# Windowed attention and gated projections: low parts of w_val summed on TensorE, x of seven groups copied to SBUF, a new order

## The chip, the cores and the metric

The kernel runs on one core of a Trainium2 chip. The core has five engines that work side by side, each with its own queue of instructions which it takes strictly in order: PE (TensorE, matrix products), DVE (VectorE), ACT (ScalarE), POOL (GpSimd) and SP, which here only issues transfers. Matrix products are written to PSUM; DVE and ACT read PSUM, and POOL's instructions in this kernel work on SBUF alone. The metric is the device time of one execution in microseconds (us), as a median of runs.

## The reference, cut to what matters

Two stages follow one another. Attention over 4 batches, 8 heads, 768 positions and head size 64, in which a query sees the first 8 keys and the 96 latest, with a bias that falls with the distance:

```python
scores = scale * np.matmul(q, k.transpose(0, 1, 3, 2))
scores = np.where(keep, scores + bias, -1000000000.0)
a = np.exp(scores - np.max(scores, axis=-1, keepdims=True))
a = a / (np.sum(a, axis=-1, keepdims=True) + 1e-09)
x = np.matmul(a, v)          # then heads side by side: x is [4, 768, 512]
```

Then a gated projection, with a causal convolution of five taps along the sequence as the gate:

```python
for k in range(K):
    gate_pre += conv_w[k] * xp[:, k:k + S, :]   # xp: x behind K - 1 rows of zeros
gate = 1.0 / (1.0 + np.exp(-gate_pre))
out = (gate * (x @ w_val)) @ w_out
```

The weights come as 64-bit floats, two 32-bit words each, and the result is float32.

## The kernel before, in words

**Groups, steps, phases.** The work is cut into 32 groups (batch, half of the sequence, pair of heads). A group has three steps of 128 queries. Four groups, the four head pairs of one half sequence, make a phase; there are eight. A group computes x transposed: 128 rows (two heads of 64) by 384 positions.

**A group's way through the engines.** `scores` (L406, PE) writes q times k. `add_bias` (L414, DVE) adds the bias and takes the minimum of the negated scores. `expo` (L424, ACT) takes the exponential and its sum. `guard` (L431, POOL or DVE), `recip` (L434, DVE) and `norm` (L439, POOL or DVE) normalise. `transpose` (L449 to L455, PE) and `evac_pt` (L149 on ACT, L151 on DVE: the helper `copy`) turn the probabilities. `pv` (L473 to L480, PE) multiplies by v into x, which has one PSUM bank (`X_B` is 1). Then all of these read x in that bank: `x_high` (a copy rounded to fp32r, L149 or L151), `x_low` (the rest, L556, DVE), five taps of the convolution into `gate` (the first at L566 on ACT or L568 on DVE, the others at L564 on DVE) and a copy of the last four positions to `hist` for the next half. `hist_in` writes four positions ahead of x (a memset at L548, or a copy from `hist`). Only when all of them are done is the bank free for the next group.

**A phase's projections.** `sigmoid` (L599, ACT), then `val` (L606): for each of four output blocks four times three products in fp32r, high by high, low by high and high by low, 384 columns each. `gated` (L613, DVE) multiplies by the gate, `g_high` and `g_low` (L619, POOL or DVE) split the product, and `outp` (L626) makes 36 products of 512 columns. `evac_o` copies the result out of PSUM and `store` (L637, SP) sends it. `val` and `outp` share two PSUM banks with the tag `moe`.

**The weights.** w_val and w_out are eight blocks of 128 by 512. Each is loaded as integers and taken apart: `f64_abs` (L305, ACT), five operations of `f64_op` on DVE (L313 clamps at F64_MIN; L315, L319, L322 and L325 work on bits and on the low word, L325 giving the remainder `r`), `w_high` (L149, rounds to fp32r), `w_rest` (L344, subtracts it) and `w_low` (L348, adds `r`), the last two on POOL or DVE.

**What sets the order.** No loop orders the queues. Each operation is added to a `Plan` with an urgency (its due time, counted in steps), a cost for each engine that may do it, and what it depends on. `Plan.order` simulates the engines: it picks for each operation that is ready the engine with the earliest end by the plan's costs plus that engine's entry in `SPARE` (L101), finds the operation that can start first, and gives its engine the most urgent one ready by then (L104). The program is written out in that order. `ring` makes an operation wait for the release of a buffer. The constants at L17 to L26 hold most urgencies: `W_AT` for the weight blocks, `U_XH`, `U_CV` and `CV_STEP` for the halves of x and the taps, `U_AM` to `U_EV` for a step's operations, `U_MOE` for the projections. `zeros` (L239) issues products that nobody reads, eight at the start (`WARM`) and one a step in the first `FILL_TO` groups. The load of group g's q and k is due at 3g - 12, of its v at 3g - 6, of a weight block 4 ahead of its `W_AT`.

Of the kernel before, what the change touches and what calls it, by code (L numbers as in the profile page):

```python
# [126 lines left out]
def attention_moe(ctx, tc, qT, kT, kg, vw, v0, v, counts_in, wv, cw, wo, out):  # L127
# [31 lines left out]
    ident = const.tile([P, P], F32, name="ident")  # L159
    rel = one.tile([P, WIN], F32, name="rel")  # L160
# [100 lines left out]
    plan.add(("IOTA",), -100, {POOL: 2.0}, iotas)  # L261

# [44 lines left out]
    def f64_op(raw, n, nm, k):  # L307
        lo, hi = raw[:, :, 0], raw[:, :, 1]
        y = T[nm, "y"][:, :n]
        yi = y.bitcast(I32)  # L310
        ve = nc.vector
        if k == 0:
            ve.tensor_scalar(out=y, in0=y, scalar1=F64_MIN, scalar2=None, op0=ALU.max)  # L313
        elif k == 1:
            ve.tensor_scalar(out=yi, in0=yi, scalar1=3, scalar2=0x3FFFFFF8,  # L315
                             op0=ALU.logical_shift_left, op1=ALU.bitwise_and)
        elif k == 2:
            h = tile_of((nm, "h"), [P, DM], I32, "wh", WT_B)[:, :n]
            ve.scalar_tensor_tensor(out=h, in0=hi, scalar=-0x40000000, in1=yi,  # L319
                                    op0=ALU.bitwise_and, op1=ALU.bitwise_or)  # L320
# [141 lines left out]
    def pv(g):  # L462
        for k in range(HB):
# [31 lines left out]
    def pv_deps(g):  # L495
        deps = [("EV", 3 * g + k) for k in range(HB)] + [("HI", g), ("LV", g)]
        return deps + ([("LV0", g)] if groups[g][1] == 0 else [])


    for g in range(NGRP + LAG):  # L500
        h = g - LAG
        if g < NGRP and g < ALONE:
            plan.add(("S", g), 3 * g, {PE: s_cost(g) + 2 * SWITCH}, lambda e, g=g: scores(g), s_deps(g))
        if 0 <= h and g < ALONE or g >= NGRP:
            plan.add(("PV", h), 3 * g, {PE: pv_cost(h) + 2 * SWITCH}, lambda e, h=h: pv(h), pv_deps(h))
        if ALONE <= g < NGRP:
            plan.add(("PV", h), 3 * g, {PE: pv_cost(h) + SWITCH}, lambda e, h=h: pv(h), s_deps(g) + pv_deps(h))
            plan.add(("S", g), 3 * g, {PE: s_cost(g) + 2 * SWITCH}, lambda e, g=g: scores(g), s_deps(g) + [("PV", h)])
            plan.follow(("S", g), ("PV", h))

    for g, (b, hf, p) in enumerate(groups):
        for k in range(HB):
# [20 lines left out]
            for j in range(2):  # L533
                plan.add(("NM", s, j), s + U_RC + 0.1, {POOL: 0.46 if full else 0.3, DVE: 0.25 if full else 0.15},
                         lambda e, s=s, j=j: norm(e, s, j), [("RC", s)])
# [7 lines left out]

    def hist_in(e, g):
        b, hf, p = groups[g]
        x = tile_of(("x", g), [P, HIST + HT], F32, "x", X_B, psum)
        if hf == 0:
            nc.vector.memset(x[:, :HIST], 0.0)  # L548
        else:
            copy(e, x[:, :HIST], hist[:, p])  # L550

    def x_high(e, g):
        copy(e, tile_of(("xh", g), [P, HT], F32R, "xh", XH_B), T["x", g][:, HIST:])

    def x_low(g):
        nc.vector.tensor_sub(tile_of(("xl", g), [P, HT], F32R, "xl", XH_B), T["x", g][:, HIST:], T["xh", g])  # L556

    def conv(e, g, k):
# [3 lines left out]
        gt, src, w = T["gate", ph][:, p], T["x", g][:, k : k + HT], cwt[:, p, k : k + 1]  # L562
# [4 lines left out]
        else:  # L567
            nc.vector.tensor_scalar(out=gt, in0=src, scalar1=w, scalar2=None, op0=ALU.mult)  # L568

    for g, (b, hf, p) in enumerate(groups):  # L570
        u = 3 * (g + LAG) + 1 + U_XE
        ph = g // NP
        key = ("HI", g)
        last = [("XL", g), ("CV", g, TAPS - 1)] + ([("HO", g)] if hf == 0 else [])
        plan.add(key, 3 * (g + LAG) - 2, {DVE: 0.08, ACT: 0.2} if hf else {DVE: 0.08}, lambda e, g=g: hist_in(e, g),
                 plan.ring("x", X_B, key, last) + ([("HO", g - NP)] if hf else []))
        if hf == 0:
            plan.add(("HO", g), u + 0.5, {ACT: 0.2, DVE: 0.08},
                     lambda e, g=g, p=p: copy(e, hist[:, p], T["x", g][:, HT:]),
                     [("PV", g)] + ([("HI", g - NP)] if g >= 2 * NP else []))  # L580
        key = ("XH", g)
        plan.add(key, u + U_XH, {ACT: 0.4, DVE: 0.47}, lambda e, g=g: x_high(e, g),
                 [("PV", g)] + plan.ring("xh", XH_B, key, [("VM", ph, NC - 1, p)]))
        key = ("XL", g)
        plan.add(key, u + U_XH + 0.1, {DVE: 0.48}, lambda e, g=g: x_low(g),
                 [("XH", g)] + plan.ring("xl", XH_B, key, [("VM", ph, NC - 1, p)]))
        for k in range(TAPS):
            key = ("CV", g, k)
            deps = [("PV", g), ("CW",)] + ([("CV", g, k - 1)] if k else [("HI", g)])
# [4 lines left out]
            plan.add(key, u + U_CV + CV_STEP * k, {DVE: 0.53} if k else {DVE: 0.53, ACT: 0.5},  # L594
# [45 lines left out]
    plan.ring("moe", 2, ("WARM",), [("WARM",)] + [("F", s) for s in range(3 * FILL_TO)])  # L640
    for ph in range(NPH):
        u = ph * PHS + U_MOE
        plan.add(("SG", ph), u - 1, {ACT: 4.0}, lambda e, ph=ph: sigmoid(ph),
                 [("CV", ph * NP + p, TAPS - 1) for p in range(NP)])
        for m in range(NC):
            for c in range(NC):
# [3 lines left out]
                plan.add(key, u + 6.0 * (4 * m + c) / 16, {PE: 0.53}, lambda e, ph=ph, m=m, c=c: val(ph, m, c), deps)  # L650
            key = ("GM", ph, m)
            plan.add(key, u + 1.5 * (m + 1), {DVE: 0.48}, lambda e, ph=ph, m=m: gated(ph, m),
# [3 lines left out]
            plan.add(key, u + 1.5 * (m + 1) + 0.2, {ACT: 0.4, DVE: 0.27}, lambda e, ph=ph, m=m: g_high(e, ph, m),  # L656
                     [("GM", ph, m)] + plan.ring("gh", 5, key, free))
            key = ("GL", ph, m)
            plan.add(key, u + 1.5 * (m + 1) + 0.3, {POOL: 0.95, DVE: 0.48}, lambda e, ph=ph, m=m: g_low(e, ph, m),
                     [("GH", ph, m)] + plan.ring("gl", 5, key, free))  # L660
        for k in range(HB):
            for c in range(NC):
# [235 lines left out]
```

## Time and profile before

| | us |
|---|---|
| median of 3 runs (317.12 to 318.05) | 317.39 |
| the profiled execution | 317.56 |
| its span, from the first to the last instruction | 315.8 |
| PE busy in the span | 282.6 |
| DVE busy | 230.2 |
| ACT busy | 230.0 |
| POOL busy | 159.2 |
| mean granted TensorE clock (1 is full speed) | 0.966 |

A profile shows one execution. Of each engine it gives the time in which it had an instruction under way; PEld is TensorE's loading of weights, which overlaps its products. Products are pipelined, so a product's own time is longer than the distance between two of them. A row of a group of instructions reads: line, engine, operation, output <- inputs, shapes, count, then busy us and mean ns of one, then the idle time of the engine before them and what ended it. A row of waits reads: who waited, for whom, us in total, how often, the longest. The chain is followed backwards from the last instruction: at each step to what released it, or to the instruction ahead of it on its engine.

### The profile page before, as it was taken

How to read it: one execution, taken by the hardware profiler on the slowest of the kernel's cores; microseconds unless marked ns; L12 is line 12 of the kernel's file. 1: busy time of each engine (PE TensorE's matmuls, PEld its weight loads, DVE VectorE, ACT ScalarE, POOL GpSimd, SP SyncE). 2: the span in 40 equal slices, each digit the busy share in tenths (PEclk: the TensorE clock that was granted, in tenths of full speed). 3: DMA queues.
4: the chain of work that ended last, by engine and by line, in shares of the span. 5: the costliest groups of instructions: out<-in, count | busy, mean ns of one | idle time of the engine just before them, and what ended most of it. 6: DMA issues, size and time to landing. Idle time of an engine off the chain costs nothing.

```text
span 315.8 us, 6866 instructions
## 1 busy us (share of the span) xinstructions
PE 282.6 (89%) x2131; PEld 225.6 (71%) x2133; DVE 230.2 (73%) x807; ACT 230.0 (73%) x643; POOL 159.2 (50%) x338
## 2 busy tenths in 40 slices
PE   7487766697999999999999999999999999999992
PEld 2254555585788778887787777888788777888981
DVE  5899889999679676787766777978676767885410
ACT  2667677977789677977797769977895779785320
POOL 5977968586335353355426443554434542750220
PEclk9769799989999999999999999999999999999997
DMA  6768655203444435332450444323443221001102
GB/s 188 267 220 258 190 172 180 85 2 85 125 138 137 120 109 179 117 86 73 137 175 26 118 138 141 119 86 92 155 147 92 67 84 70 0 3 61 41 36 75
DMA packets 21069, 36.27 MB, mean 115 GB/s; under 512 B 2592, under 2 KB 12832, under 8 KB 21024
## 3 DMA queue, kind: packets, MB, share of 16 engines
q1 hardware_dynamic: 21024, 35.75, 36.4%
q8 instruction: 19, 0.31, 0.4%
q14 instruction: 26, 0.21, 0.2%
HBM read 29.45 MB, written 6.29 MB: 113 GB/s over the span
## 4 chain that ended last, share of the span: by engine, by line
PE 40%; DVE 29%; POOL 10%; ACT 8%; issue 5%; DMA 4%; SPq 1%; POOLq 0%; ACTq 0%
PE o L626 13%; DVE gate L564 12%; PE val L606 9%; DVE t L414 7%; POOL p L439 6%; PE x L477 5%; PE x L480 3%; DVE xl L556 3%; PE s L406 3%; PE pt L452 3%; ACT gate L566 3%; PE pt L455 2%; POOL sm L431 2%; ACT p L424 2%; DMA v<-in_v 2%
## 5 line engine op out<-in xcount | busy, mean ns | idle before, releaser
L424 ACT ACTIVATE p<-t,mins 128x232 f32<-128x232 f32 (+1 forms) x192 | 90.3, 472 | 22.2 <-DVE mins L414 17.1
L439 POOL TENSOR_SCALAR p<-p,rs 128x232 f32<-128x232 f32 (+1 forms) x179 | 84.9, 487 | 33.3 <-DVE rs L434 22.9
L564 DVE SCALAR_TENSOR_TENSOR gate<-x,cwt,gate 128x384 f32<-128x384 f32 x128 | 78.1, 610 | 7.8 <-ACT gate L566 7.4
L414 DVE CUSTOM_DVE_ANT_0 t<-s,bias 128x232 f32<-128x232 f32 (+1 forms) x192 | 67.4, 371 | 0.0
L431 POOL TENSOR_SCALAR sm<-sm 128x2 f32<-128x2 f32 x92 | 20.8, 226 | 84.6 <-ACT p L424 79.5
L149 ACT COPY a<-pt 128x464 f32<-128x464 f32 (+1 forms) x90 | 46.2, 513 | 18.5 <-PE pt L455 13.7
L606 PE MATMUL val<-xh,wvh 128*128 128x384 f32 x128 | 48.0, 375 | 2.5 <-DVE g L613 2.2
L406 PE MATMUL s<-rk,rq 64*128 64x232 f32 (+1 forms) x384 | 44.9, 360 | 4.0 <-DVE ('w', 0)_y L313 2.8
L606 PE MATMUL val<-xl,wvh 128*128 128x384 f32 x128 | 44.2, 346 | 1.2 <-DVE xl L556 1.2
L626 PE MATMUL o<-woh,gh 128*128 128x512 f32 x96 | 41.4, 432 | 3.3 <-DVE g L613 3.3
L606 PE MATMUL val<-xh,wvl 128*128 128x384 f32 x128 | 44.2, 346 | 0.0
L452 PE MATMUL pt<-ident,p 104*128 104x104 f32 x160 | 33.2, 276 | 11.7 <-ACT a L149 5.2
L452 PEld LDWEIGHTS pt<-ident,p 104*128 104x128 f32 x160 | 19.6, 141 | 31.9 <-POOL p L439 16.9
L434 DVE RECIPROCAL rs<-sm 128x2 f32<-128x2 f32 x96 | 15.6, 162 | 34.6 <-POOL sm L431 33.3
L406 PEld LDWEIGHTS s<-rk,rq 64*128 64x128 f32 x384 | 32.4, 186 | 11.2 <-DVE ('w', 0)_y L313 3.3
L626 PE MATMUL o<-wol,gh 128*128 128x512 f32 x96 | 37.9, 395 | 0.0
L626 PE MATMUL o<-woh,gl 128*128 128x512 f32 x96 | 37.8, 394 | 0.0
L424 ACT ACTIVATION_READ_ACCUMULATOR p<-t,mins 128x1 f32 x192 | 36.4, 190 | 0.0
L619 POOL TENSOR_TENSOR gl<-g,gh 128x384 fp32r<-128x384 f32 x27 | 27.7, 1026 | 16.3 <-ACT gh L149 15.1
L477 PE MATMUL x<-a,v 128*64 128x128 f32 x320 | 32.5, 281 | 0.3 <-ACT a L149 0.2
L455 PE MATMUL pt<-ident,p 128*128 128x128 f32 x160 | 31.4, 278 | 0.0
L606 PEld LDWEIGHTS val<-xh,wvh 128*128 128x128 f32 x128 | 24.8, 194 | 5.2 <-DVE g L613 3.8
(150 smaller groups left out, 465.9 us busy)
## 6 DMA issues: line engine op xcount, KB each, us to landing
rq<-in_qT SPq DMA_DIRECT2D x32, 192.0 KB, 3.6
v<-in_vw SPq DMA_DIRECT2D x16, 384.0 KB, 3.2
out<-ob SPq DMA_DIRECT2D x24, 256.0 KB, 2.1
v<-in_vw SPq DMA_DIRECT2D x16, 256.0 KB, 2.8
rk<-in_kT SPq DMA_DIRECT2D x16, 252.0 KB, 3.7
rk<-in_kT SPq DMA_DIRECT2D x16, 200.0 KB, 3.1
w<-in_wv SPq DMA_DIRECT2D x4, 512.0 KB, 4.6
w<-in_wo SPq DMA_DIRECT2D x4, 512.0 KB, 4.5
```

The costliest lines, as they stand in the source:

```text
L149: nc.scalar.copy(dst, src)
L406: nc.tensor.matmul(T["s", g, k, j][:, :n], T["rq", g][r, k * P : (k + 1) * P], T["rk", g][r, c0 : c0 + n], start=True, stop=True)
L414: nc.vector.tensor_tensor_reduce(out=t[:, :n], in0=T["s", s // HB, s % HB, j][:, :n], in1=bias[:, h, :P] if n == P else bias[:, h, P:], op ...
L424: nc.scalar.activation(T["p", s][:, j, :n], T["t", s, j][:, :n], AF.Exp, bias=mins[:, s, j : j + 1], scale=-1.0, accum_out=T["sm", s][:, j ...
L439: engine(e).tensor_scalar(out=pr, in0=pr, scalar1=rs, scalar2=1.0, op0=ALU.mult, op1=ALU.mult)
L452: nc.tensor.transpose(pt[:, j * QA : (j + 1) * QA], pr[:QA, j, :P], ident[:QA, :QA])
L455: nc.tensor.transpose(pt[:, c : c + P], pr[:, j, CA:], ident)
L477: nc.tensor.matmul(head(j, P), T["v", g][:, k, j, 1], a[:, 2 * QA + j * P : 2 * QA + (j + 1) * P], start=True, stop=False)
L564: nc.vector.scalar_tensor_tensor(out=gt, in0=src, scalar=w, in1=gt, op0=ALU.mult, op1=ALU.add)
L606: nc.tensor.matmul(T["val", ph, m], (wvh, wvh, wvl)[r][:, c, m * P : (m + 1) * P], (T["xh", g], T["xl", g], T["xh", g])[r], start=(c == 0 ...
L619: engine(e).tensor_sub(tile_of(("gl", ph, m), [P, HT], F32R, "gl", 5), T["g", ph, m], T["gh", ph, m])
L626: nc.tensor.matmul(T["o", ph, k], (T["gh", ph, c], T["gl", ph, c], T["gh", ph, c])[r][:, cols], (woh, woh, wol)[r][:, c], start=(c == 0 an ...
```

## The change

It does three things. First, for w_val alone, the low part is summed by TensorE in a `moe` bank: the unit matrix (f32) times the unrounded weight, minus the unit matrix (fp32r) times the rounded one, plus it times the remainder, which is now written as fp32r; one copy out of PSUM gives wvl. The signed unit matrices are made once on ACT. The two `moe` banks thus go to the warming products, then to the four sums, then to the projections. Second, in the first seven groups x is copied from its bank to SBUF (`x_out`), and the halves, the taps and `hist` are made from that copy, of which there are eight buffers; the bank is free after the copy, and the next group's `pv` waits for the copy. Since the source is SBUF, POOL may do these groups' `hist_in`, `hist` copies, x_high, x_low and first tap too. POOL may now also do the clamp of each weight block. Third, nearly all urgencies are new, with some costs, and the filler products stop after the first group instead of the fourth. The constants:

```diff
-U_D1, RAW_B = -0.4, 4
-FILL_N, FILL_TO, U_F = 1, 4, 0.2
-W_AT = (0, 3, 6, 9, 14.5, 17, 22, 22.5)
-SPARE = {"vector": 0.6, "gpsimd": -0.2, "scalar": 0.0}
+U_D1, RAW_B = -1.85, 4
+FILL_N, FILL_TO, U_F = 1, 1, -0.88
+W_AT = (0, 3, 6, 9, 17.45, 17.58, 22, 22.5)
+SPARE = {'vector': 0.66, 'gpsimd': -0.2, 'scalar': 0.0}
-U_XE, U_XH, U_CV, CV_STEP = 0.7, -0.4, 0.5, 0.1
-U_AM, U_EX, U_RC, U_PT, U_EV, U_MOE = 0.7, 1.0, 0.5, 1.1, 2.2, 18
+U_XE, U_XH, U_CV, CV_STEP = 0.7, -0.4, 1.71, 0.21
+U_AM, U_EX, U_RC, U_PT, U_EV, U_MOE = -0.33, 1.0, 0.72, -3.96, 2.2, 18
+EARLY, XS_B, U_XO, U_CVE = 7, 8, 0.21, 0.5
+U_L, U_LV, U_WL, U_S, U_HI, U_NM = -11.64, -5.47, -2.92, -1.79, -1.49, -0.02
+U_PH = (-1.14, 0.0, 0.68, 0.0, 0.0, 0.0, 0.0, 0.0)
+U_SG, U_GM, GM_STEP, U_GH, U_GL, U_O, VAL_T, O_T, U_OE = 1.75, 0.06, 1.18, 0.2, 0.12, 6.09, 6.65, 3.63, 2.0
```

The weights:

```diff
+    def signed_units(e):
+        nc.scalar.copy(units[:, 0], ident)
+        nc.scalar.mul(units[:, 1], ident, -1.0)
...
-            ve.tensor_scalar(out=y, in0=y, scalar1=F64_MIN, scalar2=None, op0=ALU.max)
+            engine(e).tensor_scalar(out=y, in0=y, scalar1=F64_MIN, scalar2=1.0, op0=ALU.max, op1=ALU.mult)
...
-    OPS64 = (0.34, 0.34, 0.6, 0.34, 0.6)
+    OPS64 = (0.45, 0.5, 0.7, 0.5, 0.65)
...
+    def w_sum(i):
+
+        ps = tile_of(("wsum", i), [P, DM], F32, "moe", 2, psum)
+        nc.tensor.matmul(ps, ident, T[("w", i), "h"].bitcast(F32), start=True, stop=False)
+        nc.tensor.matmul(ps, units[:, 1], wvh[:, i], start=False, stop=False)
+        nc.tensor.matmul(ps, units[:, 0], T[("w", i), "r"], start=False, stop=True)
...
-            plan.add(key, u + 0.1 * k, {DVE: OPS64[k]}, lambda e, i=i, k=k: f64_op(T["w", i], DM, ("w", i), k), deps)
+            plan.add(key, u + 0.1 * k, {DVE: OPS64[k]} if k else {DVE: OPS64[k], POOL: 0.95},
+                     lambda e, i=i, k=k: f64_op(e, T["w", i], DM, ("w", i), k), deps)
...
+        if i < NC:
+            key = ("WS", i)
+            plan.add(key, u + 0.6, {PE: 1.7}, lambda e, i=i: w_sum(i),
+                     [("WH", i), ("W4", i), ("UNITS",)] + plan.ring("moe", 2, key, [("WP", i)]))
+            plan.add(("WP", i), u + 0.7, {ACT: 0.52, DVE: 0.6},
+                     lambda e, i=i: copy(e, wvl[:, i], T["wsum", i]), [("WS", i)])
+            continue
```

x of the first groups (in `hist_in`, `x_high`, `x_low`, `conv` and the `hist` copy the source becomes `x_of(g)`, and POOL may do them where g is below EARLY):

```diff
+    def x_of(g):
+        return T["xs" if g < EARLY else "x", g]
...
+    def x_out(e, g):
+        copy(e, T["xs", g][:, HIST:], T["x", g][:, HIST:])
...
-    def x_low(g):
+    def x_low(e, g):
...
+        done = ("PV", g)
+        if early:
+            plan.ring("x", X_B, ("PV", g), [("XE", g)])
+            done = ("XE", g)
+            plan.add(done, 3 * (g + LAG) + U_XO, {ACT: 0.4, DVE: 0.47}, lambda e, g=g: x_out(e, g),
+                     [("PV", g), ("HI", g)])
...
+        plan.add(key, u + U_XH, {POOL: 0.85, **xh} if early else xh, lambda e, g=g: x_high(e, g),
+                 [done] + plan.ring("xh", XH_B, key, [("VM", ph, NC - 1, p)]))
...
+        xl = {DVE: 0.5}
+        plan.add(key, u + U_XH + 0.1, {POOL: 1.0, **xl} if early else xl, lambda e, g=g: x_low(e, g),
...
+            first = {DVE: 0.53, ACT: 0.5}
+            plan.add(key, u + (U_CVE if early else U_CV) + CV_STEP * k,
+                     {DVE: 0.58 if early else 0.53} if k else {POOL: 0.75, **first} if early else first,
```

And the projections' due times:

```diff
-        u = ph * PHS + U_MOE
-        plan.add(("SG", ph), u - 1, {ACT: 4.0}, lambda e, ph=ph: sigmoid(ph),
+        u = ph * PHS + U_MOE + U_PH[ph]
+        plan.add(("SG", ph), u + U_SG, {ACT: 4.0}, lambda e, ph=ph: sigmoid(ph),
...
-            plan.add(key, u + 1.5 * (m + 1), {DVE: 0.48}, lambda e, ph=ph, m=m: gated(ph, m),
+            plan.add(key, u + U_GM + GM_STEP * m, {DVE: 0.48}, lambda e, ph=ph, m=m: gated(ph, m),
...
-                plan.add(key, u + 6 + 6.0 * (4 * k + c) / 12, {PE: 0.70}, lambda e, ph=ph, k=k, c=c: outp(ph, k, c), deps)
+                plan.add(key, u + U_O + O_T * (4 * k + c) / 12, {PE: 0.70}, lambda e, ph=ph, k=k, c=c: outp(ph, k, c), deps)
```

The loads' due times become 3g + U_L, 3g + U_LV and W_AT + U_WL, those of `scores` and `pv` 3g + U_S in place of 3g, and those of `norm` U_RC + U_NM in place of U_RC + 0.1.

More of the change, by code (lines that the diff above doesn't have):

```diff
@@ L159, in attention_moe @@
     ident = const.tile([P, P], F32, name="ident")
+    units = one.tile([P, 2, P], F32R, name="units")
     rel = one.tile([P, WIN], F32, name="rel")
@@ L261, in attention_moe @@
     plan.add(("IOTA",), -100, {POOL: 2.0}, iotas)
+    def signed_units(e):
+        nc.scalar.copy(units[:, 0], ident)
+        nc.scalar.mul(units[:, 1], ident, -1.0)
+    plan.add(("UNITS",), 0, {ACT: 0.5}, signed_units, [("IOTA",)])
     def read_counts(e):
@@ L462, in pv @@
     def pv(g):
+        if g < EARLY:
+            x_bank(g)
         for k in range(HB):
@@ L495, in pv_deps @@
     def pv_deps(g):
-        deps = [("EV", 3 * g + k) for k in range(HB)] + [("HI", g), ("LV", g)]
+        deps = [("EV", 3 * g + k) for k in range(HB)] + [("XE", g - 1) if 0 < g <= EARLY else ("LV", g), ("LV", g)]
+        deps += [("HI", g)] if g >= EARLY else []
         return deps + ([("LV0", g)] if groups[g][1] == 0 else [])
@@ L533, in attention_moe @@
             for j in range(2):
-                plan.add(("NM", s, j), s + U_RC + 0.1, {POOL: 0.46 if full else 0.3, DVE: 0.25 if full else 0.15},
+                plan.add(("NM", s, j), s + U_RC + U_NM, {POOL: 0.46 if full else 0.3, DVE: 0.25 if full else 0.15},
                          lambda e, s=s, j=j: norm(e, s, j), [("RC", s)])
@@ L561, in conv @@
             tile_of(("gate", ph), [P, NP, HT], F32, "gate", GATE_B)
-        gt, src, w = T["gate", ph][:, p], T["x", g][:, k : k + HT], cwt[:, p, k : k + 1]
+        gt, src, w = T["gate", ph][:, p], x_of(g)[:, k : k + HT], cwt[:, p, k : k + 1]
         if k:
@@ L567, in conv @@
         else:
-            nc.vector.tensor_scalar(out=gt, in0=src, scalar1=w, scalar2=None, op0=ALU.mult)
+            engine(e).tensor_scalar(out=gt, in0=src, scalar1=w, scalar2=1.0, op0=ALU.mult, op1=ALU.mult)
     for g, (b, hf, p) in enumerate(groups):
@@ L572, in attention_moe @@
         ph = g // NP
+        early = g < EARLY
         key = ("HI", g)
         last = [("XL", g), ("CV", g, TAPS - 1)] + ([("HO", g)] if hf == 0 else [])
[L575 to L576 removed]
+        hi = {DVE: 0.08, ACT: 0.2} if hf else {DVE: 0.08}
+        if early:
+            hi = {POOL: 0.15, **hi}
+            ring = plan.ring("xs", XS_B, key, last)
+        else:
+            ring = plan.ring("x", X_B, key, last)
+        plan.add(key, 3 * (g + LAG) + U_HI, hi, lambda e, g=g: hist_in(e, g), ring + ([("HO", g - NP)] if hf else []))
+        done = ("PV", g)
+        if early:
+            plan.ring("x", X_B, ("PV", g), [("XE", g)])
+            done = ("XE", g)
+            plan.add(done, 3 * (g + LAG) + U_XO, {ACT: 0.4, DVE: 0.47}, lambda e, g=g: x_out(e, g),
+                     [("PV", g), ("HI", g)])
         if hf == 0:
[L578 to L580 removed]
+            ho = {ACT: 0.2, DVE: 0.08}
+            plan.add(("HO", g), u + 0.5, {POOL: 0.15, **ho} if early else ho,
+                     lambda e, g=g, p=p: copy(e, hist[:, p], x_of(g)[:, HT:]),
+                     [done] + ([("HI", g - NP)] if g >= 2 * NP else []))
         key = ("XH", g)
[L582 to L583 removed]
+        xh = {ACT: 0.4, DVE: 0.47}
+        plan.add(key, u + U_XH, {POOL: 0.85, **xh} if early else xh, lambda e, g=g: x_high(e, g),
+                 [done] + plan.ring("xh", XH_B, key, [("VM", ph, NC - 1, p)]))
         key = ("XL", g)
[L585 removed]
+        xl = {DVE: 0.5}
+        plan.add(key, u + U_XH + 0.1, {POOL: 1.0, **xl} if early else xl, lambda e, g=g: x_low(e, g),
                  [("XH", g)] + plan.ring("xl", XH_B, key, [("VM", ph, NC - 1, p)]))
@@ L655, in attention_moe @@
             key = ("GH", ph, m)
-            plan.add(key, u + 1.5 * (m + 1) + 0.2, {ACT: 0.4, DVE: 0.27}, lambda e, ph=ph, m=m: g_high(e, ph, m),
+            plan.add(key, u + U_GM + GM_STEP * m + U_GH, {ACT: 0.4, DVE: 0.27}, lambda e, ph=ph, m=m: g_high(e, ph, m),
                      [("GM", ph, m)] + plan.ring("gh", 5, key, free))
             key = ("GL", ph, m)
-            plan.add(key, u + 1.5 * (m + 1) + 0.3, {POOL: 0.95, DVE: 0.48}, lambda e, ph=ph, m=m: g_low(e, ph, m),
+            plan.add(key, u + U_GM + GM_STEP * m + U_GL, {POOL: 0.95, DVE: 0.48}, lambda e, ph=ph, m=m: g_low(e, ph, m),
                      [("GH", ph, m)] + plan.ring("gl", 5, key, free))
```

43 lines of the change are left out of this document (22 added, 21 removed).

## The prediction

> **What bounds the kernel now.** I read the page first: its span and its busy shares in 40 slices of 7.9 us.
>
> ```profile
> span 315.8 us, 6866 instructions
> ...
> PE   7487766697999999999999999999999999999992
> PEld 2254555585788778887787777888788777888981
> DVE  5899889999679676787766777978676767885410
> ACT  2667677977789677977797769977895779785320
> POOL 5977968586335353355426443554434542750220
> PEclk9769799989999999999999999999999999999997
> ```
>
> The reader is to see two kernels in one. From the eleventh slice on (80 us) PE stands at 9 nearly throughout, and no other engine does for long. In the ten slices before it PE stands at 4 to 9, DVE at 8 or 9 nearly throughout, POOL at 5 to 9, and the granted clock dips to 0.6 to 0.8. The table of windows puts numbers on it (columns: stretch, its length, then busy us and count of PE, PEld, DVE, ACT, POOL, then clock, DMA share, GB/s):
>
> ```profile
> 0.00:80.00 80.00, 58.06 (x408) 40.66 (x412) 69.90 (x227) 55.36 (x159) 60.15 (x108) 0.89 0.52 163
> 10.00:70.00 60.00, 44.29 (x322) 32.02 (x321) 55.89 (x176) 45.03 (x130) 46.90 (x75) 0.86 0.53 167
> 80.00:310.00 230.00, 224.55 (x1725) 184.97 (x1725) 160.29 (x580) 174.48 (x484) 99.09 (x231) 1.00 0.32 100
> ```
>
> In the first 80 us, which I call the head, PE is idle 80 - 58.06 = 21.9 us; in the 230 us after it 5.5 us. DVE is busy 55.89 of 60 us (93%) between 10 and 70 us, so the head is set by DVE: there it splits the eight weight blocks and does the attention and the convolution at once. The chain of waits shows what becomes of a head that ends earlier:
>
> ```profile
> 293.87 7.31 PE val L606 x42
> 301.18 8.42 PE o L626 x36
> 309.62 0.59 ACT ob L149
> ```
>
> The last 16 us are projections alone, back to back: work that PE owes from earlier. So a microsecond of PE idleness that leaves the head leaves the end of the run as well, as long as PE stays full after it. The forecast is a sum over the head, plus a small term for the order after it.
>
> **What goes off DVE.** Three edits do that. The clamp at F64_MIN (L313) may go to POOL for all eight blocks, the first w_val subtraction (L344) leaves DVE, and seven x_low (L556) may go to POOL. The windows of L313 alone (DVE) and of L344 alone (DVE, then POOL; its w_val part lies before 40 us), and the DVE groups of the first 80 us:
>
> ```profile
> 0.00:80.00 80.00, 4.30 (x8) 0.89 0.52 163
> ```
> ```profile
> 0.00:40.00 40.00, 0.67 (x1) 3.81 (x3) 0.83 0.69 222
> ```
> ```profile
> L564 DVE SCALAR_TENSOR_TENSOR gate<-x,cwt,gate 128x384 f32<-128x384 f32 x24 | 14.6, 608 | 1.4 <-ACT gate L566 1.3
> ...
> L556 DVE TENSOR_TENSOR xl<-x,xh 128x384 fp32r<-128x384 f32 x6 | 3.3, 550 | 0.0
> ```
>
> The clamps are 4.30 us. The planner gives each to the engine with the earliest end by its own costs: POOL 0.95 - 0.2 against DVE 0.45 + 0.66, so POOL unless it is 0.36 us late. The subtraction is 0.67, and seven x_low at 0.55 are 3.85. Together 8.82 us.
>
> **What comes onto DVE, and the taps.** The new copy of x out of PSUM (x_out) goes to ACT, at 0.40 against 0.47 + 0.66, unless ACT is 0.73 us late. One costs 0.56 us on DVE and 0.48 on ACT by the same copy of x into xh:
>
> ```profile
> L149 ACT CAST xh<-x 128x384 fp32r<-128x384 f32 x25 | 11.9, 476 | 10.7 <-PE x L480 10.7
> L151 DVE CAST xh<-x 128x384 fp32r<-128x384 f32 x7 | 3.9, 556 | 3.2 <-PE x L480 3.2
> ```
>
> I put two of seven on DVE (+1.1; ends 0 and +3.9). ACT, busy 55.36 of 80 us, gets the other five and the four copies of summed low parts, under 5 us together; its idle 24.6 us hide that. The 28 later taps of these groups (L564, 608 ns) now read x from SBUF. The nearest rows with a stream from SBUF are these, with 512 columns:
>
> ```profile
> L319 DVE SCALAR_TENSOR_TENSOR ('w', 5)_h<-w,('w', 5)_y 128x512 int32<-128x512 int32 x1 | 0.7, 690 | 0.0
> L319 DVE SCALAR_TENSOR_TENSOR ('w', 7)_h<-w,('w', 7)_y 128x512 int32<-128x512 int32 x1 | 0.8, 822 | 0.0
> ```
>
> By columns that is 0.52 to 0.62 us for 384, so 28 taps move by -2.5 to +0.3 us. I take nothing, because the slower row lies nearest to what a fuller POOL would make of it. [...]
>
> DVE's sum is -8.82 + 1.1 = -7.7 us (ends -11.3 and -4.6). At the head's density, 69.90 / 80 = 0.874, the remaining 62.2 us take 71.2 us: 8.8 us less, if DVE alone decides (ends 13 and 5).
>
> **What POOL makes of it.** w_val's low parts leave POOL: three subtractions, 3.81 us above, and four additions (L348), this row:
>
> ```profile
> 0.00:40.00 40.00, 5.26 (x4) 0.83 0.69 222
> ```
>
> That is 9.07 us off. What comes on is priced from POOL's groups, in the first 80 us and then from 80 to 310 us:
>
> ```profile
> L439 POOL TENSOR_SCALAR p<-p,rs 128x232 f32<-128x232 f32 x35 | 20.6, 601 | 4.5 <-DVE rs L434 3.5 <-DVE x L548 0.4 <-PE s L406 0.4
> L431 POOL TENSOR_SCALAR sm<-sm 128x2 f32<-128x2 f32 x23 | 7.5, 325 | 4.8 <-ACT p L424 3.1
> L439 POOL TENSOR_SCALAR p<-p,rs 128x128 f32<-128x128 f32 x8 | 3.5, 454 | 0.4 <-DVE rs L434 0.3
> ...
> L619 POOL TENSOR_TENSOR gl<-g,gh 128x384 fp32r<-128x384 f32 x2 | 2.4, 1219 | 0.1
> ```
> ```profile
> L439 POOL TENSOR_SCALAR p<-p,rs 128x232 f32<-128x232 f32 x114 | 52.8, 476 | 21.1 <-DVE rs L434 15.5 <-PE pt L455 2.7 <-DVE x L548 1.4
> L619 POOL TENSOR_TENSOR gl<-g,gh 128x384 fp32r<-128x384 f32 x25 | 25.3, 1011 | 16.3 <-ACT gh L149 15.1 <-DVE rs L434 0.4
> L431 POOL TENSOR_SCALAR sm<-sm 128x2 f32<-128x2 f32 x69 | 13.3, 193 | 79.8 <-ACT p L424 76.4
> L439 POOL TENSOR_SCALAR p<-p,rs 128x128 f32<-128x128 f32 x23 | 8.4, 377 | 7.7 <-DVE rs L434 4.0 <-DVE x L548 2.2 <-DVE x L151 1.5
> ```
>
> A clamp of 512 columns, carried on along the slope of p from 128 to 232 columns, is 0.74 us by the later rows and 1.0 by the head's: eight are 5.9 to 8.0, I take 7.0. x_low has the shape of gl, 1.01 to 1.22: seven are 7.1 to 8.5, I take 7.8. First taps (384 columns, 0.62 to 0.82 us by the same slopes) may come too, none to seven; I take two, 1.5. POOL then has 60.15 - 9.07 + 7.0 + 7.8 + 1.5 = 67.4 us of work in a head that DVE alone would allow to be 71.2 us: 95%. The windows show no engine at that for so long. At DVE's present 93% POOL needs 67.4 / 0.93 = 72.5 us, at 90%, the least that a 9 on the page stands for, 74.9; I take 74. So POOL, not DVE, sets the new head, and the gain is 80 - 74 = 6 us.
>
> **PE's own changes.** A sum of w_val's low parts is one f32 product of 512 columns with the unit matrix and two in fp32r. Six f32 products of 232 columns take 1.38 us from their start to the next row:
>
> ```profile
> 40.59 1.45 PE L406 MATMUL s<-rk,rq 64*128 64x232 f32 x12
> 41.97 0.40 PE L452 MATMUL pt<-ident,p 104*128 104x104 f32 x2
> ```
>
> So 512 columns are 0.51 us, and 512 in fp32r are 8.42 / 36 = 0.23 by the chain's row: 0.97 for one sum, 3.9 for four, 6.8 by the planner's 1.7. The head's 21.9 us of idle PE hide this; with that cover gone it costs the same 3.9 to 6.8. Nine filler products fewer can let the clock dip longer: at most three more slices of 7.9 us at 0.6, in which a 70% busy PE would lose 6.6 us, most of it from time it waits anyway. I charge both to the cover, 0 in the sum, and leave 3 us for them in the range.
>
> **x's bank and the order.** PE's waits (us in total, times, longest) show what these could free:
>
> ```profile
> PE o L626 <- DVE g L613: 3.3, 6, 1.7
> PE s L406 <- DVE ('w', 0)_y L313: 2.8, 1, 2.8
> PE val L606 <- DVE g L613: 2.2, 2, 2.0
> PE x L473 <- DVE x L548: 1.8, 2, 1.6
> ```
>
> The x bank is freed after one copy now, not after the taps: 1.8 us of waits that name it, inside the head's idle time, where the next scores wait for DVE in any case; no term of its own. The 2.8 us that end with the first clamp lie in the head too, and most of them are the work that DVE does before that clamp; no term either. The gated products are due 1.4 to 2.4 steps earlier, which can take some of the 5.5 us in which PE waits for g; part of these lie after 80 us, and PE's whole idleness there is 5.5. I take -1 there, ends -3 and +3, since every queue's order is new.
>
> **Sum.** The profiled execution took 317.56 us, 1.76 outside its span; the median of the three is 317.39, 0.17 lower. 317.56 - 6 - 1 = 310.6, so 310.4 against the median.
>
> **Rivals.** *DVE alone decides* (0.18): POOL's share is hidden because the planner leaves some norms or guards to DVE or ACT takes the first taps. For it: ACT's idle 24.6 us have room for what either could do. Against it: the planner's POOL costs carry a credit of 0.2 and DVE's a charge of 0.66. The head is 8.8 to 13 us shorter: 303.5 to 308.
>
> *POOL is stretched and the gain goes* (0.17). POOL's p of 232 columns takes 601 ns in the head against 476 after it, sm 325 against 193: the head's DVE work already costs POOL 35 x 0.125 + 23 x 0.132 + 8 x 0.077 + 2 x 0.21 = 8.4 us. The 28 taps turn from one stream out of SBUF into two. With half as much again, 4.2 us, POOL needs (67.4 + 4.2) / 0.91 = 78.7; with as much again 83, and no gain is left, since a POOL that can't follow keeps its norms on DVE as now: 314 to 317.5. [...]
>
> *POOL's queue delays the attention: slower* (0.10). The fifteen new pieces of about 1 us stand in the same queue as the norms that the transposes wait for:
>
> ```profile
> PEld pt L452 <- POOL p L439: 16.9, 36, 2.0
> ```
>
> If each delays one step, 15 us come on against 7 off: 325. Half of them cancel the gain; from there on it is slower, 318.5 to 325. Against it: x_low is due 0.7 of a step behind the norms of the step it falls in, so where both are ready the norms go first.
>
> **How the numbers follow.** The forecast (0.55) covers 308 to 314 by itself. Under 0.3% (1 us) a measurement of this kernel can't tell from no change. Faster by more, below 316.4: 0.55 + 0.18 + half of the second rival, 0.09, is 0.82; within it 0.07, the rest of that rival but 0.01; slower 0.11. The range takes in the first two rivals, with the 3 us for PE's terms inside it: 303.5 to 317.5.
>
> **What would show it.** Right: PE reaches its unbroken 9s some 6 us earlier, before 75 us; POOL above 90% and DVE below 88% from 10 to 70 us; L313 and seven of 32 xl on POOL; scores of group 1 without the 2.8 us wait. Wrong: POOL's p above 650 ns in the head with longer waits of pt for it (second and third rival); PE's idleness after 80 us above 8 us (the order); more than the present four slices under 9 in PEclk (the fillers).

## The result and the profile after

The changed kernel takes 321.46 us (320.98 to 321.67), the kernel before 317.25 in the same runs: a ratio of 1.0126, with a 95% interval of 1.0104 to 1.0148. It is slower by 4 us, where 310.4 was forecast and 317.5 was the end of the range. The time lies in the span of the third rival, which had a chance of 0.10.

The page of the changed kernel, the lines that answer to those of before:

```profile
span 319.6 us, 6850 instructions
...
PE   6596886777689999999999999999999999999991
PEld 2363665665478987897789788987788778977980
DVE  4787678887758877698678876877697877995310
ACT  3596775877568977997789788967797779774220
POOL 5889999999982743454335434353435432641220
PEclk9697897899979999999999999999999999999998
```

DVE has lost its 9s in the head and POOL has taken them: eight slices in a row. PE's unbroken 9s begin two slices later than before. The windows say it in us (stretch, length, then busy of PE, PEld, DVE, ACT, POOL):

```profile
10.00:70.00 60.00, 46.48 (x303) 34.23 (x303) 46.82 (x149) 43.68 (x126) 54.72 (x76) 0.83 0.52 167
...
80.00:90.00 10.00, 6.39 (x53) 4.58 (x54) 8.19 (x26) 4.98 (x15) 9.57 (x12) 0.96 0.24 73
```
```profile
0.00:90.00 90.00, 66.23 (x438) 46.76 (x439) 68.73 (x219) 60.35 (x172) 80.25 (x126) 0.88 0.48 153
90.00:313.30 223.30, 220.53 (x1703) 184.01 (x1701) 163.78 (x587) 172.43 (x479) 93.15 (x212) 0.99 0.33 100
```

From 10 to 70 us DVE fell from 93% to 78%, as it was meant to, and POOL rose from 78% to 91%. The head now lasts about 89 us, since between 80 and 90 us PE still waits and POOL is at 96%. The same two windows of the kernel before, up to its last product at 309.6 us:

```profile
0.00:90.00 90.00, 68.04 (x488) 48.57 (x491) 76.12 (x252) 63.17 (x183) 64.03 (x118) 0.91 0.52 162
90.00:309.50 219.50, 214.49 (x1645) 177.06 (x1643) 154.07 (x556) 166.29 (x460) 95.21 (x220) 1.00 0.32 97
```

In the first 90 us PE is idle 23.8 us, before 22.0; after that 2.8, before 5.0. So the new order after the head is better by 2.2 us. The loss lies in the head: at 90 us PE still has 220.53 us of work to do, before 214.49. POOL has 80.25 us of work there, before 64.03. Two groups of rows make that. The first is the clamp, one row for each block:

```profile
L324 POOL TENSOR_SCALAR ('w', 0)_y<-('w', 0)_y x1: 1965/1965/1965, 9.8 to 9.8; 128x512 f32<-128x512 f32 x1
...
L324 DVE TENSOR_SCALAR ('w', 2)_y<-('w', 2)_y x1: 424/424/424, 23.1 to 23.1; 128x512 f32<-128x512 f32 x1
L324 POOL TENSOR_SCALAR ('w', 3)_y<-('w', 3)_y x1: 1918/1918/1918, 31.4 to 31.4; 128x512 f32<-128x512 f32 x1
L324 POOL TENSOR_SCALAR ('w', 4)_y<-('w', 4)_y x1: 2330/2330/2330, 43.5 to 43.5; 128x512 f32<-128x512 f32 x1
```

On DVE it took 0.42 us, on POOL 1.92 to 2.33. The second is p, first on POOL up to 90 us, and beside it the early taps on DVE up to 80 us:

```profile
L466 POOL TENSOR_SCALAR p<-p,rs 128x232 f32<-128x232 f32 x38 | 28.4, 756 | 2.2 <-DVE rs L461 1.4 <-PE pt L482 0.4 <-PE pt L476 0.4
...
L466 POOL TENSOR_SCALAR p<-p,rs 128x128 f32<-128x128 f32 x7 | 4.7, 679 | 0.5 <-PE pt L482 0.4
```
```profile
L603 DVE SCALAR_TENSOR_TENSOR gate<-xs,cwt,gate 128x384 f32<-128x384 f32 x21 | 16.4, 779 | 0.4 <-POOL gate L607 0.3
```

p of 232 columns went from 601 to 756 ns, the taps from 608 to 779. And PE's waits up to 92 us show who pays:

```profile
PE pt L479 <- POOL p L466: 8.3, 11, 2.4
PE pt L476 <- POOL p L466: 4.1, 3, 2.8
...
PE val L662 <- POOL xl L595: 2.9, 1, 2.9
```

The rows of the kernel before that answer to the first two, over the same stretch:

```profile
PE pt L452 <- POOL p L439: 2.4, 3, 1.8
...
PE pt L449 <- POOL p L439: 0.9, 1, 0.9
```

PE's waits for p went from 3.3 to 12.4 us. With the wait for x_low, POOL stands behind 15.3 us of them in the changed kernel, most of what PE waits for in the head.

### The profile page after: what moved, and what is told of

Its sections match the earlier page's. It is cut to its first block, busy times and chain, and to the rows that moved or that the text cites. A ratio compares the mean times of both kernels' runs of the same rounds, so it can differ in the third digit from the quotient of the medians.

```text
span 319.6 us, 6850 instructions
## 1 busy us (share of the span) xinstructions
PE 286.8 (90%) x2140; PEld 230.8 (72%) x2140; DVE 232.5 (73%) x806; ACT 232.8 (73%) x650; POOL 173.4 (54%) x337
## 4 chain that ended last, share of the span: by engine, by line
PE 59%; DVE 14%; POOL 13%; ACT 4%; issue 4%; DMA 3%; SPq 1%; POOLq 0%; ACTq 0%
PE o L682 16%; PE val L662 15%; PE s L433 7%; POOL p L466 7%; PE x L506 5%; DVE gate L603 5%; PE pt L479 4%; PE pt L482 4%; PE x L509 4%; DVE t L441 3%; PE pt L476 2%; DMA w<-in_wv 2%; ACT p L451 2%; PE x L502 1%; DVE xl L595 1%
## 5 line engine op out<-in xcount | busy, mean ns | idle before, releaser
L466 POOL TENSOR_SCALAR p<-p,rs 128x232 f32<-128x232 f32 (+1 forms) x164 | 85.8, 534 | 32.4 <-DVE rs L461 17.0
L441 DVE CUSTOM_DVE_ANT_0 t<-s,bias 128x232 f32<-128x232 f32 (+1 forms) x192 | 69.6, 373 | 0.1
L603 DVE SCALAR_TENSOR_TENSOR gate<-x,cwt,gate 128x384 f32<-128x384 f32 x100 | 61.4, 614 | 5.6 <-ACT gate L605 5.3
L458 POOL TENSOR_SCALAR sm<-sm 128x2 f32<-128x2 f32 x88 | 19.3, 219 | 77.3 <-ACT p L451 72.3
L662 PE MATMUL val<-xh,wvh 128*128 128x384 f32 x128 | 46.9, 367 | 2.2 <-DVE g L669 2.2
L675 POOL TENSOR_TENSOR gl<-g,gh 128x384 fp32r<-128x384 f32 x30 | 30.3, 1010 | 18.5 <-ACT gh L153 17.9
L479 PEld LDWEIGHTS pt<-ident,p 104*128 104x128 f32 x160 | 20.5, 145 | 27.4 <-POOL p L466 14.7
L482 PE MATMUL pt<-ident,p 128*128 128x128 f32 x160 | 32.2, 283 | 0.0
L509 PE MATMUL x<-a,v 104*64 104x104 f32 x320 | 28.8, 258 | 0.0
```

The source lines that it names most:

```text
L441: nc.vector.tensor_tensor_reduce(out=t[:, :n], in0=T["s", s // HB, s % HB, j][:, :n], in1=bias[:, h, :P] if n == P else bias[:, h, P:], op ...
L466: engine(e).tensor_scalar(out=pr, in0=pr, scalar1=rs, scalar2=1.0, op0=ALU.mult, op1=ALU.mult)
L479: nc.tensor.transpose(pt[:, j * QA : (j + 1) * QA], pr[:QA, j, :P], ident[:QA, :QA])
L482: nc.tensor.transpose(pt[:, c : c + P], pr[:, j, CA:], ident)
L509: nc.tensor.matmul(head(j, QA), T["v", g][:CA, k, j, 0], a[:CA, j * QA : (j + 1) * QA], start=False, stop=True)
L603: nc.vector.scalar_tensor_tensor(out=gt, in0=src, scalar=w, in1=gt, op0=ALU.mult, op1=ALU.add)
```

## Experiments

Three theories stood at the start. One: POOL sets the head, and the clamp is what overfills it. Two: POOL is held up by the taps, which now read two streams from SBUF. Three: the new order of the queues costs.

**One word of the clamp.** The maximum becomes a multiplication by 1, so the clamp is left out; every queue stays as it is.

```diff
-            engine(e).tensor_scalar(out=y, in0=y, scalar1=F64_MIN, scalar2=1.0, op0=ALU.max, op1=ALU.mult)
+            engine(e).tensor_scalar(out=y, in0=y, scalar1=1.0, scalar2=1.0, op0=ALU.mult, op1=ALU.mult)
```

> The changed kernel with one word different: the clamp of each weight block multiplies by 1 in place of taking the maximum with F64_MIN (so the clamp is left out), on the same engine and in the same place of every queue. Theory 1 (POOL sets the head and the clamp is what overfills it: 1.92 to 2.33 us each on POOL, where p's rows gave 0.74 to 1.0): the seven clamps on POOL take 0.7 to 1.1 us, POOL has 7 to 9 us less in the head, and the time falls from 321.5 to 312.5 to 315. Theory 2 (the clamp is a side matter; POOL is held up by the taps that now read two streams from SBUF): the rows of p stay at 740 ns or more in the head, and the time falls by 3 us at most, to 318.5 or more. Theory 3 (the new order is what costs, in the head and after it): 320 or more.

Measured: 313.17 us, 0.9856 of the kernel before (0.9838 to 0.9873). Two of its clamps on POOL:

```profile
L324 POOL TENSOR_SCALAR ('w', 3)_y<-('w', 3)_y x1: 617/617/617, 29.7 to 29.7; 128x512 f32<-128x512 f32 x1
L324 POOL TENSOR_SCALAR ('w', 4)_y<-('w', 4)_y x1: 1029/1029/1029, 40.5 to 40.5; 128x512 f32<-128x512 f32 x1
```

Each of the seven is shorter by 1.3 us, 9.1 together, and the time falls by 8.3: nearly the whole of POOL's work comes off the end. That is what a bound is. PE's waits for p fell from 12.4 to 6.0 us. Theory one holds; two and three can't have brought these 8.3 us, since p of 232 columns stays at 755 ns here (739 in the changed kernel, both up to 80 us) and the order is the same.

**The clamp on DVE, in the same order.** The plan still counts it as POOL's, and it is issued to DVE at that place.

```diff
-            engine(e).tensor_scalar(out=y, in0=y, scalar1=F64_MIN, scalar2=1.0, op0=ALU.max, op1=ALU.mult)
+            ve.tensor_scalar(out=y, in0=y, scalar1=F64_MIN, scalar2=1.0, op0=ALU.max, op1=ALU.mult)
```

> The changed kernel in its own order of every queue but for one thing: where the planner gave a clamp to POOL, it is issued to DVE, at that place of the order. POOL loses seven clamps of 1.92 us and DVE gets seven of 0.43. Theory 1 (POOL overfilled by the clamps, and the slow time of the run with replanned queues comes from its other order): 311 to 315, near the run with the multiplication. Rival (clamps on DVE are what made the replanned run slow, since DVE and POOL hold each other up): 319 to 324, as there.

Measured: 312.00 us, 0.9836 (0.9813 to 0.9859): faster than both kernels, with the whole computation. Its windows from 0 to 90 us, from there to the last product, and from 10 to 70 us:

```profile
0.00:90.00 90.00, 74.78 (x503) 53.40 (x503) 75.65 (x244) 66.52 (x190) 71.16 (x129) 0.92 0.51 163
90.00:304.70 214.70, 212.10 (x1640) 177.02 (x1638) 159.30 (x570) 165.80 (x461) 88.22 (x201) 1.00 0.33 99
10.00:70.00 60.00, 50.75 (x354) 37.84 (x354) 53.56 (x165) 48.13 (x137) 49.40 (x77) 0.91 0.54 177
```

DVE is at 89% and POOL at 82%: neither is overfilled. PE is idle 17.8 us in these two windows, 27.0 in the kernel before, while it works 4.4 us more (286.9 against 282.5). 9.2 less 4.4 is 4.8, the difference of the two spans.

**The clamp alone in the kernel before.** POOL is offered the clamps at 0.95 and takes five; in the second run they multiply by 1, with the queues of the first.

```diff
-            ve.tensor_scalar(out=y, in0=y, scalar1=F64_MIN, scalar2=None, op0=ALU.max)
+            engine(e).tensor_scalar(out=y, in0=y, scalar1=F64_MIN, scalar2=1.0, op0=ALU.max, op1=ALU.mult)
...
-            plan.add(key, u + 0.1 * k, {DVE: OPS64[k]}, ...
+            plan.add(key, u + 0.1 * k, {DVE: OPS64[k]} if k else {DVE: OPS64[k], POOL: 0.95}, ...
```

> The kernel before with one edit: the clamps offered to POOL as well, at the cost of 0.95 that the change gives them. Theory 1: POOL gets up to eight clamps of 1.92 us, 60 + 15 us of work in a head of 80, and the time rises to 319 to 324 by this edit alone. Theory 2: DVE loses 4 us and POOL has room while the taps read PSUM: 313 to 316. Theory 3: within 1 us of 317.3.

> The kernel before with the clamps offered to POOL, as in the earlier run of 324.2 us, but multiplying by 1 in place of the maximum (the clamp is left out); the order is that run's. Theory 1: the 6.5 us that the clamps cost go back by what POOL gains, some 8 clamps at 1.3 us, so 314 to 318. Rival (the moved places in the order cost, not POOL's time): 321 or more.

Measured: 324.19 us, 1.0199 (1.0175 to 1.0224), and 319.34, 1.0075 (1.0044 to 1.0107): 6.5 and 2.2 us above the kernel before in the same runs. The clamps took this long in the first:

```profile
L313 POOL TENSOR_SCALAR ('w', 3)_y<-('w', 3)_y x1: 1917/1917/1917, 30.5 to 30.5; 128x512 f32<-128x512 f32 x1
```

and 0.62 in the second: 5 x 1.3 = 6.5 us of POOL's time for 4.3 us of the end. Without x copies or any other part of the change, this one edit costs 6.5 us. 4.3 of them come with the clamp's time; the other 2.2 stay with the new order and five pieces of 0.62 us on POOL, which weren't parted. The second run ended above its expectation; the rival had a share.

The profiles show how the loss gets to the end here, and it is hardly by idleness: PE is idle 34.1, 33.4 and 33.2 us in the first run, the second and the kernel before, but busy 288.1, 283.8 and 282.6 with the same products, at a mean granted clock of 0.941, 0.963 and 0.966. So the loss shows as products that take longer, and not as longer waits in all. The lower clock fits that as the reason; it isn't tested.

**Which forms are dear on POOL.** Each block on POOL has its clamp in another form, so the weights aren't the reference's.

```diff
+            s1, s2, o1, o2 = {
+                0: (1.0, F64_MIN, ALU.mult, ALU.max), 1: (F64_MIN, None, ALU.max, None),
+                3: (F64_MIN, 0.0, ALU.max, ALU.add), 4: (1.0, None, ALU.mult, None),
+                5: (1.0, 0.0, ALU.mult, ALU.add), 6: (100.0, 1.0, ALU.min, ALU.mult), 7: (F64_MIN, 1.0, ALU.subtract, ALU.mult),
```

> The changed kernel with each block's clamp in another form, so its weights aren't the reference's: block 0 multiplies, then takes the maximum; 1 takes the maximum alone; 3 maximum, then adds 0; 4 one multiplication alone; 5 multiplies, then adds 0; 6 minimum, then multiplies; 7 subtracts, then multiplies; each on POOL. If the maximum itself is dear there, blocks 0, 1, 3 and 6 take 1.5 us or more and blocks 4, 5 and 7 0.6 to 1.1. If it is the pair of unlike operations, block 1 falls to about 0.6 and 5 and 7 rise to 1.9.

The pairs of operations, and the single ones:

```profile
L332 POOL TENSOR_SCALAR ('w', 0)_y<-('w', 0)_y x1: 1975/1975/1975, 9.6 to 9.6; 128x512 f32<-128x512 f32 x1
...
L332 POOL TENSOR_SCALAR ('w', 5)_y<-('w', 5)_y x1: 918/918/918, 54.3 to 54.3; 128x512 f32<-128x512 f32 x1
L332 POOL TENSOR_SCALAR ('w', 6)_y<-('w', 6)_y x1: 1944/1944/1944, 67.5 to 67.5; 128x512 f32<-128x512 f32 x1
L332 POOL TENSOR_SCALAR ('w', 7)_y<-('w', 7)_y x1: 1930/1930/1930, 79.2 to 79.2; 128x512 f32<-128x512 f32 x1
```
```profile
L330 POOL TENSOR_SCALAR ('w', 1)_y<-('w', 1)_y x1: 1498/1498/1498, 16.6 to 16.6; 128x512 f32<-128x512 f32 x1
L330 POOL TENSOR_SCALAR ('w', 4)_y<-('w', 4)_y x1: 1915/1915/1915, 43.1 to 43.1; 128x512 f32<-128x512 f32 x1
```

Neither expectation was right. Pairs with a maximum, a minimum or a subtraction all took 1.93 to 1.98 us, and a maximum alone 1.50. Blocks 4 and 5 lie in places that lengthen the piece, so their values are estimates. Block 4's place adds 0.41 in the two other runs (2330 against 1918, 1029 against 617), so one multiplication alone is also about 1.50. Block 5's place adds 0.30 in them (2223 against 1918, 914 against 617), so a multiplication followed by an addition is about 0.62. Of these forms only that one and the pair of multiplications were quick. p and the bias tiles were already written as a pair of multiplications.

**The taps.** The 28 later taps of the early groups are left out of the version of 312.0 us, so their gates miss four of five taps.

```diff
+        if k and g < EARLY:
+            return
```

> The version of 312.0 us (the change's order, clamps issued to DVE) without the 28 later taps of the first seven groups, so their gates miss four of five taps; all else stands in its place. It is run for one row: p of 232 columns on POOL in the first 80 us, 717 ns with the taps from SBUF, 601 in the kernel before with the taps from PSUM. If the taps' two streams out of SBUF stretch POOL, p falls to 620 or less; if the weights' operations or POOL's own pieces do, it stays above 680. The time, with 22 us of DVE work gone from the head, is between 300 and 310 either way.

Measured: 304.59 us in one run, and p of 232 columns up to 80 us, first here, then in the version of 312.0 with its taps:

```profile
L466 POOL TENSOR_SCALAR p<-p,rs 128x232 f32<-128x232 f32 x42 | 25.1, 609 | 4.5 <-DVE rs L461 2.9 <-PE pt L482 1.5
```
```profile
L466 POOL TENSOR_SCALAR p<-p,rs 128x232 f32<-128x232 f32 x36 | 25.4, 717 | 6.5 <-DVE rs L461 6.4
```

So theory two holds as a cost, not as the cause: the taps from SBUF stretch each p by 0.11 us; without them it is near the 601 of the kernel before. 22 us of DVE time went as well (28 x 0.78). The time is 7.4 us under 312.0, and by the kernel before in the same runs (318.74 here, 317.17 there) it is 9.0. How much of that is p's and how much DVE's isn't parted.

**x_low on DVE as well**, in the same order:

```diff
-        engine(e).tensor_sub(tile_of(("xl", g), ...
+        nc.vector.tensor_sub(tile_of(("xl", g), ...
```

> The changed kernel in its own order with the clamps and all x_low issued to DVE: POOL loses six more pieces of 1.2 us, DVE gets six of 0.62. If POOL is still the bound without the clamps, 1 to 4 us less than the run with only the clamps on DVE; if DVE is the bound again, 1 to 4 us more; within 1 us if they balance.

313.00 us, 0.9871 (0.9838 to 0.9903), which can't be told from 312.00: DVE and POOL balance there.

**Orders planned anew.** The clamps offered to DVE alone; and that without x copies (`EARLY` is 0).

```diff
-            plan.add(key, u + 0.1 * k, {DVE: OPS64[k]} if k else {DVE: OPS64[k], POOL: 0.95},
+            plan.add(key, u + 0.1 * k, {DVE: OPS64[k]},
```

> The changed kernel with the clamps offered to DVE alone, as before the change; the planner orders anew. Theory 1: POOL loses 14 us of work in the first 90, DVE gets 4 back, and the time is 311 to 315, the forecast's gain. Theory 2: 317 to 320. Theory 3: 320 or more.

> The changed kernel with no early groups (x stays in its PSUM bank in all of them) and the clamps offered to DVE alone: what is left are the sums of the low parts on PE and the new order. Theory 1: between the kernel before and the run with the clamps on DVE and the copies, 313 to 317, since POOL loses 9 us but DVE loses only one subtraction. Theory 2: faster than that run, 310 to 314, as no tap reads x from SBUF. Theory 3: slower than before, 319 or more.

Measured: 323.55 us, 1.0171 (1.0117 to 1.0225), and 322.94, 1.0158 (1.0138 to 1.0179). The first missed what theory one expected, though it gives each clamp to the same engine as the version of 312.0: 11.6 us lie between two orders, with some other pieces on other engines too (four x_low on POOL here, six there). So the second run can't be read as the worth of the copies, and no run here shows that worth alone. In the slow order DVE fills up for a stretch while PE works little, at a low clock:

```profile
60.00:70.00 10.00, 5.55 (x25) 4.21 (x21) 10.00 (x27) 7.05 (x17) 5.44 (x7) 0.67 0.23 72
```

That this stretch makes the whole difference isn't shown. Five runs asked why the orders differ so much. In the first the planner is told the clamp's measured price on POOL. In the second, with the clamps on DVE alone, it is told the prices of p, the guard, x_low and the early taps in the head. The third has those prices with the clamps planned on POOL and issued to DVE. In the last two the planner's charge on DVE (`SPARE`) is moved a little, for the version of 312.0 and for the kernel before. The first three, cut to the prices:

```diff
-{DVE: OPS64[k], POOL: 0.95}
+{DVE: OPS64[k], POOL: 1.92}
...
-{POOL: 0.16, DVE: 0.1}
+{POOL: 0.3 if s < 27 else 0.16, DVE: 0.1}
-{POOL: 0.46 if full else 0.3, DVE: 0.25 if full else 0.15}
+{POOL: (0.72 if full else 0.63) if s < 27 else (0.46 if full else 0.36), DVE: 0.25 if full else 0.15}
-{POOL: 1.0, **xl} if early
+{POOL: 1.2, **xl} if early
-{DVE: 0.58 if early else 0.53} if k else
+{DVE: 0.72 if early else 0.53} if k else
```

> The changed kernel with the planner's cost of a clamp on POOL set to the measured 1.92 in place of 0.95; the queues are ordered anew by that. If a right price is all that the planner needs, it keeps most clamps off POOL and the time is near that of the same order with the clamps on DVE, 311 to 315. If the other urgencies fit one order alone, a replanned order loses several us however well it is priced: 318 to 325.

> The changed kernel with clamps offered to DVE alone, and the planner's prices in the head set to what the runs showed: p on POOL 0.72 and 0.63, guard 0.3, x_low 1.2, early taps 0.72. The urgencies stay. If wrong prices made the replanned order of 323.6 us slow, 311 to 315. If the urgencies fit one order alone, 317 or more.

> The same prices, but the plan still gives clamps to POOL at 0.95 where it likes, and they are issued to DVE, as in the version of 312.0 us. If prices are what matters, within 2 us of the run before it in this call. If the slot that stays empty on POOL is what made 312.0, 310 to 314 here and 317 or more there. If neither, both are 317 or more, and the order of 312.0 is one that the urgencies were fitted to.

> The version of 312.0 us (the change's order, clamps issued to DVE) with the planner's charge on DVE at 0.68 in place of 0.66, which moves a few dozen instructions in the queues and no work between kernels. If the order is worth much by itself, 314 to 320; if it is not, within 1 us of 312.

> The kernel before with the planner's charge on DVE at 0.62 in place of 0.6, which moves some hundreds of instructions in the queues and changes nothing else. If the order is worth much by itself, 319 to 325; if it is not, within 1 us of 317.3.

Measured, with the ratios to the kernel before: 318.41 us, 1.0018 (0.9999 to 1.0037); 315.46, 0.9920 (0.9894 to 0.9946); 315.35, 0.9913 (0.9883 to 0.9942); with the charge moved, 312.45 in two runs, 0.9826 (0.9781 to 0.9872), and 318.16, 1.0010 (0.9990 to 1.0031).

The clamp's price alone isn't enough: the planner still puts two clamps on POOL at 1.92 us, and the time falls at the near end of the 318 to 325 expected if the urgencies fit one order alone. All the prices together move the replanned order from 1.017 to 0.992. That lies in the gap between the two expectations of the second run. The third came within 0.2 us of it, as expected if prices are what matters, so keeping a slot free on POOL does nothing that can be told. A few dozen or some hundred moved instructions do nothing that can be told either. What parts 0.992 from 0.984 wasn't settled.

## Why the prediction was wrong, point by point

**What bounds the head.** POOL after the change: right, since 8.3 us came back when POOL's pieces alone got shorter. DVE before it is read from its 93%; no run takes work off DVE alone in that kernel. That the end moves as PE's idleness in the head does is right only in part. Of the 8.1 us between the two spans 5.3 are idle time of PE; 2.8 are its busy time for the same products, 286.8 against 284.0. And the head grew by some 9 us, the time by 4, since PE did more of its work inside the longer head: 65.28 us up to 89 us, before 58.06 up to 80. The wait ahead of group 1's scores, which was to go, stayed: 2.9 us, now for a bias on DVE.

**What goes off DVE.** Right in kind: -7.7 us by the sum, and the head's DVE work fell from 69.90 to 60.54 us in the first 80 us, part of it because less was reached. Seven of eight clamps and six of seven x_low went to POOL, and one x_out came to DVE instead of two.

**What POOL makes of it: the step that failed.** The term for the clamps was half of what they took. "A clamp of 512 columns, carried on along the slope of p from 128 to 232 columns, is 0.74 us by the later rows and 1.0 by the head's: eight are 5.9 to 8.0, I take 7.0." Seven took 14.2. The slope was that of another form: the multiplication put in the clamp's place took 0.62 to 1.03 us, close to the 0.74 to 1.0. The trace of before has no maximum on POOL, so both ends of that bound came from one kind of row, and the range was too narrow by what the form could cost. The run with multiplications has the forecast's own price of a clamp and takes 313.2 us: 8.3 of the 11.1 us that the forecast was off are this term. The other 2.8 aren't parted between the terms below. With the clamps off POOL altogether the kernel takes 312.0, inside the range too. Nor is it so that no engine is seen at 95% for long: the rows have PE at 98% for 230 us behind the head, and POOL reached 96% from 80 to 90 us.

**The second rival's price** stood in the range and not in the sum, and POOL's rows show it in full: p of 232 columns at 756 ns in place of 601 is 38 x 0.155 = 5.9 us, p of 128 another 1.6 (679 against 454), 7.5 together. The rival took 4.2 and 8.4. What this costs in time isn't measured alone; the run with multiplications has nearly the same stretch of p and is 2.8 us over the forecast. One source of it is shown: in the version of 312.0 us p took 717 ns with the later taps and 609 without them, both up to 80 us. 67.4 + 7.2 + 7.5 is 82 us, and POOL's rows give 80.25. That they come so close is in part chance: of what was counted, five x_low in place of seven and three first taps in place of two fell in these 90 us, and two copies x_high came that weren't counted.

**The taps on DVE.** Taken as no change; they went from 608 to 747 ns (779 for the 21 up to 80 us), 28 x 0.14 = 3.9 us. The median tap from SBUF took 618 ns, one from PSUM 615 in the same execution; the mean is raised by single ones of up to 1745, like the one beside POOL's subtraction below.

**PE's own changes.** One sum took 1.32 us at full clock (block 3, below), not 0.97, and two took 2.4 and 2.6 us at a granted clock of 0.53 and 0.50: 7.8 for the four, where 6.8 was the most allowed. PE was busy 4.2 us more in all (286.8 against 282.6), while its idleness stayed as it was. That isn't the price of the sums alone, since PE's busy time for the same products is 284.0 in the run with multiplications and 286.9 in the version of 312.0, at mean granted clocks of 0.966 and 0.972, so the clock isn't all of it either; no run shows what the sums cost by themselves. The clock dipped in six slices, before in four, but in three with the same fillers in the version of 312.0, so fewer fillers alone don't bring the dips.

**The order after the head.** -1 by the sum, -2.2 by PE's idleness there.

**The third rival** had its mechanism: the norms stood behind new pieces in POOL's queue, and the waits for p grew from 3.3 to 12.4 us. It counted fifteen pieces of 1 us; there were seven of 1.9 to 2.3 us, six x_low of 1.2 and three first taps of 0.9, and its span of 318.5 to 325 holds the time. Its chance was set low, though the sum for POOL stood at 95% of the head with no price in it for p's longer time.

## What to carry to other kernels

Before work is moved to an engine, find in the trace that very operation on that engine; a row of the same shape with another operation is no bound (here 0.62 us for a pair of multiplications, 1.92 for the clamp). POOL at 78% of a stretch had little room, and a sum that fills an engine has to be made at the slower rows: p took 609 ns on POOL without the later taps on DVE and 717 with them. The planner's order depended on its prices: with the measured ones it won back 8 us of what the replanned order had lost. So an experiment on placement is read only with the order held fixed.

## What the runs showed of the hardware

On POOL a pair of multiplications over 128x512 f32 took 0.62 to 0.66 us and a pair with a maximum, a minimum or a subtraction 1.92 to 1.98, but for the places that lengthened the piece (0.91 to 1.03, and 2.22 to 2.33); a maximum alone took 1.50. The sum of one block's low parts on PE at full clock:

```profile
40.15 1.02 PE L364 MATMUL wsum<-('w', 3)_h,ident 128*128 128x512 f32 x2
40.61 0.80 PE L365 MATMUL wsum<-wvh,units 128*128 128x512 f32 x1
41.24 0.39 PE L366 MATMUL wsum<-('w', 3)_r,units 128*128 128x512 f32 x1
41.47 0.34 PE L662 MATMUL val<-xh,wvh 128*128 128x384 f32 x1
```

From start to start, the f32 product (two rows of the trace) took 0.46 us, the first one in fp32r behind it 0.63 and the second 0.23. In block 1, also at full clock, the first two are 0.46 and 0.64. The 0.4 that the first in fp32r took beyond the second is the main part of what the forecast's 0.97 left out; that the change of form costs it is read from these rows, not tested. And one tap took 1.75 us beside a subtraction on POOL (changed kernel):

```profile
53.81 1.75 DVE L603 SCALAR_TENSOR_TENSOR gate<-xs,cwt,gate 128x384 f32<-128x384 f32 x1
53.86 1.27 POOL L355 TENSOR_TENSOR ('w', 4)_h<-('w', 4)_h,woh 128x512 f32<-128x512 f32 x1
```

The tap, 0.62 us in the median, ends 0.43 us after a POOL subtraction with two inputs that began just behind it. That the subtraction held it is read from these two rows, not tested.
